# Linear attention with a gated feed-forward: wo's parts loaded a round ahead, the query pass's loads in written order, and the last product in two sets of columns

## Chip, cores and metric

The kernel runs on one core of a Trainium2 chip. The metric is the device time of one execution in microseconds (us); smaller is better. Times are compared as medians of several runs, and one further execution was recorded by the hardware profiler.

## The reference

S = 2048 tokens, D = 1024, H = 32 heads of 32, F = 3584, all in fp32.

```python
xn = layernorm(x)
q, k, v = heads(xn @ wqkv)
phi_q = concat(softmax(q @ w_phi), softmax(-q @ w_phi))      # per head, phi_k alike
kv  = einsum("bhsf,bhsd->bhfd", phi_k, v);  z = sum over s of phi_k
o   = (phi_q @ kv) / (phi_q @ z + 1e-6)
s   = o @ wo
g   = silu((silu(xn @ w1) * (xn @ w3)) @ w2)
out = x + s * g
```

## The kernel before

Every large product runs on TensorE (PE) in a reduced-width fp32 form. Each operand is split into a high and a low half, `split()`: ACT casts the high half (line 92), DVE subtracts to get the low half (line 93). A product is then three passes, high by high, high by low, low by high (`PASSES`, line 88). Two-by-two blocks are multiplied with seven products instead of eight (`ORDER`, line 59): A11, A12, S2, S1, S3, S4, A22, which accumulate in three PSUM banks a, b and c. Each of the seven is 12 matmuls of 128x512 here. Bank b is used by A11, S2, S3 and A22 one after the other, and c by S1 and S4, and the partial sums in between are read out of the bank. So PE's S2 waits for ACT's copy of A11, S3 for ACT's copy of S2, S4 for ACT's copy of S1, and A22 for DVE's addition after S3 or S4.

The stages follow one another: layer norm and the gate and up products with side work (to about 1117 us; the products of line 666), two K/V passes (c = 0 and 1, `heads`, products of line 951, to 1452 us), the query pass (c = 2, `query_heads` and `query_product`, line 1025, to about 1605 us), the down product (line 1430, to 2143 us) and the attention with the output product (`attend`, `out_half`, line 1594, to the end).

A K/V pass and the query pass have eight rounds each (`pos`), one for each pair of token tiles. A round is the seven products; after each of them (steps j = 0 to 6) the generator `steps()` issues side work:

- at j = 0 the seven operands `xo` of the next round, 512 KB each (`reload`, line 629);
- in the K/V passes one of 16 parts of wo, by `wo_split(c, k, j, halves)`: at j = 0 the load of the raw part from the input (`wo_raw`, 256 KB, line 1208), at j = 4 its split into two `wo_half`, at j = 6 their stores to `wo_d` in DRAM (line 1214);
- in some rounds the fetches of the next pass's weights, 2 MB each (`fetch`, line 169: `op3B`, `op3T` and so on);
- in the query pass the first loads of w2 (`bo`, `load_b`, line 1166) at the places named in `B_LOADS`.

In `heads`, k is copied out of bank b by ACT (line 957), v's parts by ACT (968 after S2, 972 after S1), then added by DVE (line 974 after S4); `kv_run` accumulates K'V in the bank `pkv` (line 907), by 64 small products between S2 and S1 of the next round. `kv_out` transposes the result by DVE into `kvz` (line 1128), and gives back two steps that are run at the ends of later products: `store` (lines 1139 and 1142) and `turned`, the small product `pz` (line 1133). In `query_heads` ACT copies q out of the banks (line 1093), POOL and DVE subtract the maxima and minima (lines 994 and 995), ACT takes the exponentials (998) and issues the store of the features to `e_d` (999). `rho_out` (line 1032) stores rho of a round, the ratios of its feature sums.

Order: in the K/V and query passes only PE's order is the written one (`in_order(ENG.PE)`); ACT, DVE, POOL and SP are placed by the framework's scheduler. From the last query round on, all engines are in written order. Loads and stores are issued mostly by SP, the feature stores by ACT.

The output product takes, for each of 16 token tiles, two halves of 512 columns with 24 matmuls of 128x512 each. A half is multiplied by the gate by DVE (`gate_mul`, line 1602), added to x (`gate_add`, line 1606; by GpSimd, and for the last tile by DVE) and stored (`store_out`, line 1610).

Of the kernel before, what the change touches and what calls it, by code (L numbers as in the profile page):

```python
# [27 lines left out]
def tile_kernel(ctx: ExitStack, tc: tile.TileContext, x, wkT, wqT, wv, wphi, wo, w1, w3, w2, out):  # L28
# [1006 lines left out]
    def query_last(i, xo, wb):  # L1035

        bank, rho, q, feats, late = {}, small.tile([P, 2, 2, 16], F, name="rho"), {}, {}, []
        parts = first_parts(ahead.pop(0))

        def kept(n, pb):  # L1040
            q[n] = work.tile([P, 512], F, name="q", tag="w")
            nc.scalar.copy(q[n], pb)

        def added(n, pb, j, c, room):
            nc.vector.tensor_add(q[n], pb, q[n])
            feats[n] = query_features(i, j, c, q.pop(n), rho, nc.gpsimd, room, True)
            feats[n][0]()

        for b, an, bn in ORDER:
            pb = query_product(bank, b, an, bn, xo, wb)  # L1050
            if an == "A11":
                kept("00", pb)
                ahead[1] = load_h(0, 1)
            elif an == "A12":
                early = e_room()
                added("00", pb, 0, 0, early[:, 0])
                next(parts)
            elif an == "S2":
                kept("01", pb)
                feats["00"][1]()  # L1060
                feats["00"][2]()
                ready.append(next(parts))
                parts = second_parts(*ready[0])
            elif an == "S1":
                kept("11", pb)
                next(parts)
            elif an == "S3":
                added("11", pb, 1, 1, early[:, 1])
                next(parts)
            elif an == "S4":  # L1070
                room = e_room()
                added("01", pb, 0, 1, room[:, 0])
                feats["11"][1]()
                ready.append(next(parts))
                parts = first_parts(ahead.pop(1))
                next(parts)
            else:
                feats["10"] = query_features(i, 1, 0, pb, rho, nc.vector, room[:, 1], True)
                feats["10"][0]()
        return {1: lambda: (ready.append(next(parts)), feats["11"][2]()), 3: lambda: feats["01"][1](), 5: lambda: feats["10"][1](),  # L1080
                7 + 5: lambda: feats["01"][2](),
                14 + 5: lambda: (feats["10"][2](), rho_out(i, rho), feats.clear())}

    def query_heads(i, first, xo, wb, steps):

        bank, rho = {}, small.tile([P, 2, 2, 16], F, name="rho")
        for b, an, bn in ORDER:
            pb = query_product(bank, b, an, bn, xo, wb)
            if late_z:
                z_add(late_z.pop())  # L1090
            if an in ("A11", "S2", "S1"):
                t = work.tile([P, 512], F, name="q", tag="w")
                nc.scalar.copy(t, pb)
                if an == "A11":
                    q00 = t
                elif an == "S2":
                    q01 = t
                else:
                    q11 = t
            elif an == "A12":  # L1100
                nc.vector.tensor_add(q00, pb, q00)
                early = e_room()
                query_features(i, 0, 0, q00, rho, nc.gpsimd, early[:, 0])
            elif an == "S3":
                nc.vector.tensor_add(q11, pb, q11)
                query_features(i, 1, 1, q11, rho, nc.gpsimd, early[:, 1])
            elif an == "S4":
                nc.vector.tensor_add(q01, pb, q01)
                late = e_room()
                query_features(i, 0, 1, q01, rho, nc.gpsimd, late[:, 0])  # L1110
            else:
                query_features(i, 1, 0, pb, rho, nc.vector, late[:, 1])
                rho_out(i, rho)
            if an == "S1" and first:
                kv_run(*pend)
                pend[2].clear()
                rooms_ev.clear()
                out_now.extend(kv_out(1, pkv))
            next(steps)
            if out_now and not first:  # L1120
                out_now.pop()()

    def kv_out(c, pkv):
        kvz = work.tile([P, 512], F, name="kvz", tag="w")
        kva, zt, zs = kvz[:, :8 * DH], kvz[:, 8 * DH:], zsum[1:]
        zsum.clear()
        for n in range(2):
            nc.vector.transpose(kva[:, P * n:P * n + P].rearrange("p (m d) -> p m d", d=DH), pkv[:, :, DH * n:DH * n + DH])

        def turned():  # L1130
            pz = ps.tile([P, 512], F, name="pz", tag="kv", bufs=1)
            for n in range(4):
                nc.tensor.matmul(pz[32 * n:32 * n + 32, :256], ones, zs[n // 2][:, n % 2 * 256:n % 2 * 256 + 256],
                                 start=True, stop=True, skip_group_check=True)
            nc.vector.tensor_scalar_add(zt[:64], pz[:64, :256], 1e-6)
            nc.vector.tensor_copy(zt[64:], pz[64:, :256])

        def store():
            nc.sync.dma_start(kv_d[:, :, :, c].rearrange("j f s m d -> (j f) s (m d)"),
                              kva.rearrange("p (s n) -> p s n", s=2))  # L1140
            for n in range(4):
                nc.sync.dma_start(z_d[n // 2, c].rearrange("(a g) n -> a (g n)", a=2)[n % 2:n % 2 + 1], zt[32 * n:32 * n + 1])

        return [store, turned]

# [54 lines left out]
    BANKS = {"a": 2, "b": 3, "c": 2}  # L1202
    pend = None
    ready, ahead = [], {}
    def wo_split(c, k, j, halves):
        if j == 0:
            halves.append(work.tile([P, 512], F, name="wo_raw", tag="w"))
            nc.sync.dma_start(halves[0], wo[k * P:(k + 1) * P, c * 512:(c + 1) * 512])
        elif j == 4:
            halves.extend(work.tile([P, 512], R, name="wo_half", tag="w") for _ in range(2))  # L1210
            split(halves[1], halves[2], halves[0])
        elif j == 6:
            for u in range(2):
                nc.sync.dma_start(wo_d[c][k][:, u], halves[1 + u].bitcast(F))

    in_order(ENG.PE)
    B_LOADS = ((3, 5), (4, 2), (4, 5), (5, 2), (5, 5), (6, 1), (6, 3), (6, 5))
    NEXT = ({0: 2, 1: 3, 2: 4, 3: 5, 4: 6}, {0: 2, 1: 3, 2: 4, 3: 5, 6: 6}, {})
    for c in range(3):
        wbn, last = {}, c == 2  # L1220
        if last:
            close("spare")
            bpa = pool("ra", 1, side="right")
        order = range(len(pairs))[::-1] if c == 1 else range(len(pairs))
        for pos, i in enumerate(order):
            nxt, end = {}, pos + 1 == len(pairs)

            def steps():
                halves = []
                for j in range(7):  # L1230
                    if j == 0:
                        if pos in (3, 4) and not last:
                            wbn.update(fetch(3 + c, pos - 3))
                        if not end:
                            nxt.update(reload(order[pos + 1]))
                    if not last:
                        wo_split(c, pos, j, halves)
                    if last and (pos, j) in B_LOADS:
                        m = B_LOADS.index((pos, j))
                        load_b(0, m // 2, (m % 2,))  # L1240
                    if end and j in NEXT[c]:
                        wbn.update(fetch(3 + c, NEXT[c][j]))
                    if last and pos + 2 == len(pairs) and j == 5:
                        ahead[0] = load_h(0, 0)
                    yield

            if last and end:
                in_order(ENG.SP, ENG.PE, ENG.Activation, ENG.DVE, ENG.Pool)
                late_features = query_last(i, xo, wb)
            elif last:  # L1250
                query_heads(i, pos == 0, xo, wb, steps())
            else:
                pend = heads(pos == 0, end, end and c == 1, xo, wb, steps(), pend)
            xo = xo if end else nxt
# [361 lines left out]
    for t in range(NT):  # L1616
# [31 lines left out]
        store_out(t, 0)  # L1648
        if count:
            lows.append(attend(t + 1, 0, count))  # L1650
        prev = out_half(t, 1, lambda: count and lows.append(attend(t + 1, 1, count)))
        for c in range(2):
            if count:
                lows[c].pop(0)()
            if t + 4 >= EARLY:
                z_sums(t + 4, c)
        lows = sum(lows, [])
    gate_mul(NT - 1, 1, prev)
    gate_add(NT - 1, 1, True)
    store_out(NT - 1, 1)  # L1660
    in_order()
    close("ps4", "rb", "acc", "q", "work", "small", "misc", "ra", "rw", "edge_r", "edge_l")

# [34 lines left out]
```

## Time and profile before

| | us |
|---|---|
| median of 3 runs | 2351.45 (2351.18 to 2353.81) |
| profiled execution | 2350.86 |
| span of its trace | 2349.1 |
| mean granted PE clock | 0.998 |
| PE's idle time before line 951's and 1025's products, and pz | 6.9 |
| last matmul's start to the end of the span | 4.8 |

The profiled execution is longer than its span by 1.8 us, the start and end that the trace does not show. The idle time in the fifth row is the sum of the waits that the list of PE's waits shows for those lines. In the profile's lists, "PE bankb L951 <- ACT k L957: 3.5, 1, 3.5" reads: PE's matmuls of line 951 into bank b waited for ACT's operation of line 957, 3.5 us in total, once, the longest 3.5. In a timeline a row is the start, the duration, the engine, the line, the operation with what it writes and reads, and the number of instructions in the group. A row of windows has, after the stretch and its length, the busy time of PE, weight loads, DVE, ACT and POOL with their counts, then the granted PE clock, the DMA engines' busy share and GB/s.

### The profile page before, as it was taken

What the parts mean: (1) busy time and instruction counts of PE and PEld (TensorE: products, weight loads), DVE (VectorE), ACT (ScalarE), POOL (GpSimd) and SP (SyncE); (2) the same over time, 40 slices, a digit from 0 to 9 for tenths busy, and PEclk for the clock granted to TensorE, in tenths of its full rate; (3) what the DMA queues carried; (4) which work ended last, traced back from release to release, by engine and by line L of the source; (5) the groups of instructions that cost most, each with busy time, mean ns of one, the idle gap of its engine ahead of it and who ended that gap; (6) DMA issues with size and microseconds to landing.
All of it is one profiled execution on the core that took longest, in us unless ns stands there. A gap on an engine that the chain in (4) does not pass through costs nothing.

```text
span 2349.1 us, 33851 instructions
## 1 busy us (share of the span) xinstructions
PE 2323.7 (99%) x12730; PEld 1900.2 (81%) x12730; DVE 1821.3 (78%) x2852; ACT 888.8 (38%) x1561; POOL 257.0 (11%) x208
## 2 busy tenths in 40 slices
PE   8999999999999999999999999999999999999999
PEld 6878877788888888888787887878888888887887
DVE  8878788885688888874577777778688888887784
ACT  6445444443345555543222122334433333353000
POOL 1000000000000000000000000332022222211652
PEclk9999999999999999999999999999999999999999
DMA  3456799997778888876978878996634554379863
GB/s 128 160 194 224 244 305 370 346 321 222 239 283 309 298 287 296 293 243 220 372 263 284 299 257 319 322 355 234 214 132 157 199 186 135 130 251 275 237 184 104
DMA packets 302740, 580.94 MB, mean 247 GB/s; under 512 B 24680, under 2 KB 156912, under 8 KB 299888
## 3 DMA queue, kind: packets, MB, share of 16 engines
q1 hardware_dynamic: 296240, 555.70, 70.2%
q10 hardware_dynamic: 6336, 23.07, 2.4%
q8 instruction: 100, 1.64, 0.3%
q14 instruction: 64, 0.52, 0.1%
HBM read 375.78 MB, written 202.91 MB: 246 GB/s over the span
## 4 chain that ended last, share of the span: by engine, by line
PE 89%; DMA 6%; DVE 2%; ACT 1%; issue 0%; POOL 0%; SPq 0%; ACTq 0%; POOLq 0%
PE bankb L666 26%; PE bankc L666 13%; PE bankb L1430 13%; PE bankc L1430 6%; PE bankb L951 6%; PE banka L666 6%; PE pm L1594 5%; PE banka L1430 3%; PE bankc L951 3%; PE bankb L1025 2%; PE banka L951 1%; DMA acc<-e_d 1%; DMA wo_raw<-in_wo 1%; PE bankc L1025 1%; DMA h_d<-h 1%; PE pkv L907 1%
## 5 line engine op out<-in xcount | busy, mean ns | idle before, releaser
L93 DVE TENSOR_TENSOR bo<-rw,bo 128x512 fp32r<-128x512 f32 x329 | 226.0, 688 | 145.9 <-ACT bo L92 145.6
L1430 PE MATMUL bankb<-bo,as 128*128 128x512 f32 x960 | 235.2, 389 | 0.0
L92 ACT CAST bo<-rw 128x512 fp32r<-128x512 f32 x329 | 202.3, 618 | 22.9 <-DMA wkv_d0B<-w2o 4.6
L1430 PEld LDWEIGHTS bankb<-bo,as 128*128 128x128 f32 x960 | 180.2, 188 | 37.7
L994 POOL TENSOR_TENSOR eq<-q,mm 128x512 f32<-128x512 f32 x24 | 25.2, 1050 | 1523.4 <-DVE mm L992 1495.5
L666 PE MATMUL bankb<-op0S,bo 128*128 128x512 f32 x672 | 166.7, 397 | 3.6 <-ACT u L702 2.8
L666 PE MATMUL bankc<-op0S,bo 128*128 128x512 f32 x672 | 162.1, 390 | 0.0
L666 PE MATMUL bankb<-op1S,bo 128*128 128x512 f32 x672 | 161.3, 389 | 0.0
L666 PE MATMUL bankc<-op1S,bo 128*128 128x512 f32 x672 | 161.3, 389 | 0.0
L666 PE MATMUL bankb<-op0A,bo 128*128 128x512 f32 x672 | 159.3, 391 | 1.1 <-ACT op0A L765 0.8
L1594 PE MATMUL pm<-wos,oT 128*128 128x512 f32 x672 | 158.3, 392 | 1.1 <-issue 0.9
L1430 PE MATMUL bankc<-bo,as 128*128 128x512 f32 x624 | 158.5, 389 | 0.2 <-DVE acc L1444 0.2
L666 PE MATMUL bankb<-op1A,bo 128*128 128x512 f32 x672 | 157.9, 390 | 0.0
L666 PEld LDWEIGHTS bankb<-op0S,bo 128*128 128x128 f32 x672 | 126.2, 190 | 36.4 <-issue 4.9
L1594 PEld LDWEIGHTS pm<-wos,oT 128*128 128x128 f32 x672 | 125.4, 188 | 29.4 <-issue 2.2
L666 PEld LDWEIGHTS bankb<-op1A,bo 128*128 128x128 f32 x672 | 125.8, 188 | 28.1 <-DVE u L710 2.1
L666 PEld LDWEIGHTS bankc<-op0S,bo 128*128 128x128 f32 x672 | 125.6, 188 | 27.3 <-issue 1.2
L666 PEld LDWEIGHTS bankb<-op0A,bo 128*128 128x128 f32 x672 | 125.4, 188 | 27.5 <-ACT op0A L765 1.0
L666 PEld LDWEIGHTS bankc<-op1S,bo 128*128 128x128 f32 x672 | 126.1, 188 | 26.2
L666 PEld LDWEIGHTS bankb<-op1S,bo 128*128 128x128 f32 x672 | 126.1, 188 | 26.2
L1430 PEld LDWEIGHTS bankc<-bo,as 128*128 128x128 f32 x624 | 117.0, 188 | 24.9 <-DVE acc L1444 0.6
L717 ACT ACTIVATE h<-bankb 128x512 f32<-128x512 f32 x56 | 33.5, 598 | 236.8 <-PE bankb L666 236.8
(291 smaller groups left out, 4394.6 us busy)
## 6 DMA issues: line engine op xcount, KB each, us to landing
rw<-in_w SPq DMA_DIRECT2D x112, 512.0 KB, 5.5
hr<-h_d SPq DMA_DIRECT2D x56, 512.0 KB, 5.5
h_d<-h SPq DMA_DIRECT2D x108, 256.0 KB, 5.7
xoS<-xo_d0S SPq DMA_DIRECT2D x44, 512.0 KB, 5.4
xoS<-xo_d1S SPq DMA_DIRECT2D x44, 512.0 KB, 5.5
xoA<-xo_d0A SPq DMA_DIRECT2D x33, 512.0 KB, 5.9
xoA<-xo_d1A SPq DMA_DIRECT2D x33, 512.0 KB, 5.1
e_d<-eq ACTq DMA_DIRECT2D x32, 512.0 KB, 6.6
```

Of the source, the lines that this page charges most:

```text
L92: nc.scalar.copy(hi, src)
L93: (by or nc.vector).tensor_sub(lo, src, hi.bitcast(F))
L666: nc.tensor.matmul(bank[b], bos[tb, f][bn][:, w, k], ao[an][:, u, k], start=first and n == 0, stop=LAST[b] == an and n == 11, skip_group_c ...
L717: nc.scalar.activation(h1, bank["b"], AF.Silu)
L907: nc.tensor.matmul(pkv[sl, m], v[:, 4 * m + h], e[:, :, 4 * m + h], start=first and m == 0, stop=last, skip_group_check=True)
L951: nc.tensor.matmul(bank[b], xo[an][:, u, k], wb[bn][:, w, k], start=an in ("A11", "A12", "S1") and n == 0, stop=LAST[b] == an and n == 11, ...
L994: eng.tensor_sub(e[:, 0], p3, mm[:, 0, :].unsqueeze(2).to_broadcast([P, 16, DH]))
L1025: nc.tensor.matmul(bank[b], xo[an][:, u, k], wb[bn][:, w, k], start=an in ("A11", "A12", "S1") and n == 0, stop=LAST[b] == an and n == 11, ...
L1430: nc.tensor.matmul(bank[b], t[:, u, pos + k], bos[kb, bn, k][:, w], start=first and n == 0, stop=LAST[b] == an and n == 5, skip_group_chec ...
L1594: nc.tensor.matmul(p, oTs[t, h][:, a, k], wos[c, 4 * h + k][:, b], start=n == 0, stop=n == 3 * ND - 1)
```

## The change

1. wo's parts. Part n + 1 is loaded at j = 4 of round n (parts 0 and 1 at j = 3 and 4 of round 0), split at j = 1 and stored at j = 2 of its own round, so that the load stands most of a round ahead of the split. Part 0 is split at j = 5 and stored at j = 6 of round 1.
2. The query pass. SP is put in written order together with PE. The w2 loads are no longer single parts at the places of `B_LOADS` but pairs at j = 5 of rounds 2 to 5. The store of rho is put after the next round's S4 (in the last round after S1). `kv_out` gives back four steps instead of two, so that its store comes two products later and `turned` stays where it was.
3. The last half of the last tile. It is done as two sets of 24 matmuls of 256 columns, each with its own multiplication, addition and store of 128 KB.

```diff
@@ query_last, query_heads
             elif an == "S1":
+                rho_out(*rhos.pop())
                 kept("11", pb)
...
+            if an == "S4" and rhos:
+                rho_out(*rhos.pop())
...
                 query_features(i, 1, 0, pb, rho, nc.vector, late[:, 1])
-                rho_out(i, rho)
+                rhos.append((i, rho))
@@ kv_out
-        return [store, turned]
+        return [store, lambda: None, lambda: None, turned]
@@ wo_split and the passes
-    def wo_split(c, k, j, halves):
-        if j == 0:
-            halves.append(work.tile([P, 512], F, name="wo_raw", tag="w"))
-            nc.sync.dma_start(halves[0], wo[k * P:(k + 1) * P, c * 512:(c + 1) * 512])
-        elif j == 4:
-            halves.extend(work.tile([P, 512], R, name="wo_half", tag="w") for _ in range(2))
-            split(halves[1], halves[2], halves[0])
-        elif j == 6:
-            for u in range(2):
-                nc.sync.dma_start(wo_d[c][k][:, u], halves[1 + u].bitcast(F))
+    wo_raws = {}
+
+    def wo_part(n):
+        return wo[n % 8 * P:(n % 8 + 1) * P, n // 8 * 512:(n // 8 + 1) * 512]
+
+    def wo_split(n, j):
+        new, now = ({3: 0, 4: 1} if n == 0 else {4: n + 1}).get(j), (((1, n),) if n else ()) + (((5, 0),) if n == 1 else ())
+        if new is not None and new < 16:
+            wo_raws[new] = [work.tile([P, 512], F, name="wo_raw", tag="w")]
+            nc.sync.dma_start(wo_raws[new][0], wo_part(new))
+        for at_, m in now:
+            if j == at_:
+                wo_raws[m].extend(work.tile([P, 512], R, name="wo_half", tag="w") for _ in range(2))
+                split(wo_raws[m][1], wo_raws[m][2], wo_raws[m][0])
+            elif j == at_ + 1:
+                raw_part, hi, lo = wo_raws.pop(m)
+                for u, h in enumerate((hi, lo)):
+                    nc.sync.dma_start(wo_d[m // 8][m % 8][:, u], h.bitcast(F))
...
-    B_LOADS = ((3, 5), (4, 2), (4, 5), (5, 2), (5, 5), (6, 1), (6, 3), (6, 5))
...
+            in_order(ENG.PE, ENG.SP)
...
-                        wo_split(c, pos, j, halves)
-                    if last and (pos, j) in B_LOADS:
-                        m = B_LOADS.index((pos, j))
-                        load_b(0, m // 2, (m % 2,))
+                        wo_split(8 * c + pos, j)
+                    if last and 1 < pos < 6 and j == 5:
+                        load_b(0, pos - 2)
@@ the last product
-        prev = out_half(t, 1, lambda: count and lows.append(attend(t + 1, 1, count)))
+        prev = None if last else out_half(t, 1, lambda: count and lows.append(attend(t + 1, 1, count)))
...
-    gate_mul(NT - 1, 1, prev)
-    gate_add(NT - 1, 1, True)
-    store_out(NT - 1, 1)
+    for u in range(2):
+        cs = slice(512 + 256 * u, 768 + 256 * u)
+        p = ps.tile([P, 512], F, name="pm", tag="mm", bufs=3)[:, :256]
+        n = 0
+        for k in range(ND):
+            for a, b in PASSES:
+                nc.tensor.matmul(p, oTs[NT - 1, k // 4][:, a, k % 4], wos[1, k][:, b, 256 * u:256 * u + 256], start=n == 0, stop=n == 3 * ND - 1)
+                n += 1
+        g, xr = gs[NT - 1][:, cs], xrs[(NT - 1) % 2][:, cs]
+        nc.vector.tensor_mul(g, p, g)
+        nc.vector.tensor_add(g, g, xr)
+        nc.sync.dma_start(out[(NT - 1) * P:, cs], g)
```

How instructions stand now is shown at three places. A row is a line, an operation, and what it writes and reads; "x2" is two alike in a row. ACT from round 0 to round 1 of the first K/V pass (`wo_half` is a part's high half, `k` the copy of A11, the copies into `ev` at 968 and 972 those of S2 and S1), before:

```order
L972 COPY ev<-bankc 128x512
L114 ACTIVATE ev<-ev 128x1024
L92 CAST wo_half<-wo_raw 128x512
L957 COPY k_9993<-bankb 128x512
L968 COPY ev<-bankb 128x512
L972 COPY ev<-bankc 128x512
L114 ACTIVATE ev<-ev 128x1024
```
and after the change:

```order
L972 COPY ev<-bankc 128x512
L114 ACTIVATE ev<-ev 128x1024
L957 COPY k_9989<-bankb 128x512
L92 CAST wo_half<-wo_raw 128x512
L968 COPY ev<-bankb 128x512
L972 COPY ev<-bankc 128x512
L114 ACTIVATE ev<-ev 128x1024
```
The cast stood ahead of the copy of k of round 1; now it stands between that copy and the copy of S2.

SP at the end of the first K/V pass, rounds 6 and 7 (`op3T` and `op3B` are the 2 MB fetches, `xoS` and `xoA` reloads, `wo_d` the stores of a split part), before:

```order
L629 DMA xoA_11201<-xo_d1A_94 128x1024
L629 DMA xoA_11203<-xo_d1A_95 128x1024
L629 DMA xoS_11205<-xo_d1S_96 128x1024
L169 DMA op3T_11035<-wkv_d2T_117 128x4096
L1208 DMA wo_raw<-in_wo 128x512
L169 DMA op3T_11061<-wkv_d2T_118 128x4096
L169 DMA op3T_11112<-wkv_d2T_119 128x4096
L169 DMA op3B_11128<-wkv_d2B_120 128x4096
L169 DMA op3T_11147<-wkv_d2T_121 128x4096
L1214 DMA wo_d_7_133<-wo_half 128x512 x2
```
and after the change:

```order
L1219 DMA wo_raw<-in_wo 128x512
L629 DMA xoS_10873<-xo_d1S_99 128x1024
L629 DMA xoA_10875<-xo_d1A_100 128x1024
L629 DMA xoA_11203<-xo_d1A_94 128x1024
L629 DMA xoA_11205<-xo_d1A_95 128x1024
L629 DMA xoS_11207<-xo_d1S_96 128x1024
L169 DMA op3T_11035<-wkv_d2T_117 128x4096
L169 DMA op3T_11065<-wkv_d2T_118 128x4096
L1227 DMA wo_d_7_133<-wo_half 128x512 x2
L169 DMA op3T_11118<-wkv_d2T_119 128x4096
L169 DMA op3B_11134<-wkv_d2B_120 128x4096
L1219 DMA wo_raw<-in_wo 128x512
```
The load of part 7 has left the fetches and stands five rows and more ahead of them; part 8's load now stands between them, and the stores of part 7 have moved ahead of the last three fetches.

SP in rounds 2 and 3 of the query pass (`bo` are w2's parts, `rho_d` the store of rho), before:

```order
L629 DMA xoA_13123<-xo_d1A_94 128x1024
L1166 DMA bo<-w_d0B_143 128x1024
L629 DMA xoA_13125<-xo_d1A_95 128x1024
L1166 DMA bo<-w_d0B_143 128x1024
L629 DMA xoS_13127<-xo_d1S_96 128x1024
L629 DMA xoS_13129<-xo_d1S_97 128x1024
L1166 DMA bo<-w_d0T_144 128x1024
L629 DMA xoS_13131<-xo_d1S_98 128x1024
L1166 DMA bo<-w_d0T_144 128x1024
L629 DMA xoS_13133<-xo_d1S_99 128x1024
L1166 DMA bo<-w_d0T_145 128x1024
L1032 DMA rho_d<-rho 128x2x32
```
and after the change:

```order
L1032 DMA rho_d<-rho 128x2x32
L1171 DMA bo<-w_d0B_142 128x1024 x2
L629 DMA xoA_13129<-xo_d1A_94 128x1024
L629 DMA xoA_13131<-xo_d1A_95 128x1024
L629 DMA xoS_13133<-xo_d1S_96 128x1024
L629 DMA xoS_13135<-xo_d1S_97 128x1024
L629 DMA xoS_13137<-xo_d1S_98 128x1024
L629 DMA xoS_13139<-xo_d1S_99 128x1024
L629 DMA xoA_13141<-xo_d1A_100 128x1024
L1032 DMA rho_d<-rho 128x2x32
L1171 DMA bo<-w_d0B_143 128x1024 x2
L629 DMA xoA_13291<-xo_d1A_94 128x1024
```
The single loads that lay between reloads are pairs behind seven reloads and the store of rho.

More of the change, by code (lines that the diff above doesn't have):

```diff
@@ L1082, in query_last @@
                 14 + 5: lambda: (feats["10"][2](), rho_out(i, rho), feats.clear())}
+    rhos = []
     def query_heads(i, first, xo, wb, steps):
@@ L1228, in steps @@
             def steps():
-                halves = []
                 for j in range(7):
```

## The prediction

> **What bounds the kernel now.** I first read the busy shares: TensorE (PE) works 2323.7 of 2349.1 us, so only time in which PE stands still, and time behind its last product, can be won. Then the waits of PE, sorted by what ended them (line; us in total, times, longest), for the lines that the change touches:
>
> ```profile
> PE 2323.7 (99%) x12730; PEld 1900.2 (81%) x12730; DVE 1821.3 (78%) x2852; ACT 888.8 (38%) x1561; POOL 257.0 (11%) x208
> ...
> PE bankb L951 <- ACT k L957: 3.5, 1, 3.5
> PE bankb L951 <- DVE ev L974: 1.3, 2, 0.7
> PE bankb L1025 <- ACT q L1093: 0.8, 1, 0.8
> PE bankc L1025 <- ACT q L1093: 0.7, 1, 0.7
> PE pz L1133 <- DVE kvz L1128: 0.4, 1, 0.4
> ```
>
> These are one wait in the K/V passes for ACT's copy of k, two for DVE, one before the first pz, two in the query pass: 3.5 + 1.3 + 0.8 + 0.7 + 0.4 = 6.7 us of idle time. A wait costs PE more than its idle time where matmuls behind it also run stretched, so I priced each by the distance between starts in PE's timeline (start, us, then the group). The yardstick is a query round without a wait, 1492.46 to 1511.50 below: 19.04 us for 7 products of 12 matmuls, 2.72 us each and 226.7 ns per matmul.
>
> **Part 1, wo's loads one round ahead.** The largest wait is in round 1 of the first K/V pass (the page's timeline, one window with PEclk as the second last but one column, and the chain of waits):
>
> ```profile
> 1140.79 2.88 PE L951 MATMUL banka<-op2B,xoA 128*128 128x512 f32 x12
> 1147.18 4.54 PE L951 MATMUL bankb<-op2T,xoS 128*128 128x512 f32 x12 [3.50 <-ACT k L957]
> 1151.64 1.10 PE L907 MATMUL pkv<-ev 128*32 128x64 f32 x64
> 1292.38 2.88 PE L951 MATMUL bankb<-op3T,xoS 128*128 128x512 f32 x12
> 1295.19 1.10 PE L907 MATMUL pkv<-ev 128*32 128x64 f32 x64
> ...
> 1145.00:1150.00 5.00, 2.82 (x7) 2.25 (x8) 3.62 (x6) 1.10 (x2) 0.00 (x0) 0.70 1.00 331
> ...
> 1136.81 9.19 DMA wo_raw<-in_wo
> 1146.02 0.62 ACT wo_half L92
> ```
>
> S2 was due at 1140.79 + 2.72 = 1143.51; an undisturbed S2 is followed by pkv after 1295.19 - 1292.38 = 2.81, so pkv was due at 1146.32. It started at 1151.64: 5.32 us lost, 3.67 by the late start and 1.65 because S2's twelve matmuls took 4.46 us (granted clock 0.70 in that window). The chain says why: the load of wo_raw goes out at 1136.81 and lands 9.19 us later, and ACT's cast of it (L92) stands in ACT's order ahead of the copy of k (L957) that empties bank b. In the changed order the copy of k stands ahead of the cast, so the whole 5.32 us should go. The Trainium skill, "TensorE: Matmul & The Clock Gate", part on the HAM clock gate, has the clock halve after a window of about 3.4 us with too little work; the 0.70 behind an idle of 3.50 us agrees, and by that rule a gap cut to 2 us would already save the stretched matmuls too.
>
> The wait moves: the cast of part 1 now stands ahead of L968, the copy of S2, for which S3 waits. Two loads go out where one did; at the window's 331 GB/s the second 256 KB land 0.79 us after 1146.00, at 1146.8. Cast 0.62 and copy of about 0.6 end at 1148.0. S3 is due 3.88 us after pkv (1295.19 to 1299.07 below), at 1150.2: 2.2 us to spare. If both landed 3 us later, 0.8 would be lost. I take nothing here. Round 1 also splits two parts, so DVE has a second subtraction of 0.69: I take 0.3 lost, between 0 and 0.7.
>
> The last rounds of both K/V passes have the same cast behind the 2 MB fetches of the next operands:
>
> ```profile
> 1277.33 2.88 PE L951 MATMUL bankb<-op2T,xoS 128*128 128x512 f32 x12
> 1286.94 2.88 PE L951 MATMUL bankb<-op3B,xoA 128*128 128x512 f32 x12
> 1299.07 2.88 PE L951 MATMUL bankb<-op3T,xoS 128*128 128x512 f32 x12
> 1307.23 2.88 PE L951 MATMUL bankb<-op3B,xoA 128*128 128x512 f32 x12
> ...
> 1268.48 10.64 DMA wo_raw<-in_wo
> 1279.85 0.69 DVE wo_half L93
> ...
> 1442.37 2.88 PE L951 MATMUL bankb<-op3T,xoS 128*128 128x512 f32 x12
> 1452.06 0.65 PE L907 MATMUL pkv<-ev 128*32 128x64 f32 x32
> 1433.53 10.38 DMA wo_raw<-in_wo
> ```
>
> Pass 0: S3 to the next A11 took 9.61 us, undisturbed 8.16: 1.45 lost. Pass 1: S3 to pkv took 9.69 instead of 8.16 + 0.09: 1.44 lost. In both, wo_raw needed over 10 us, and DVE's half of the split (L93) came late into the chain that ends in L974, which empties the bank for A22. In the change part 7's load is issued in round 6, ahead of the fetches, and part 15's likewise; the split then stands where nothing waits for a DMA. I take all of 1.45 + 1.44. The pz wait goes too: DVE's transposes of kvz stand ahead of L974 in the changed order, 0.4.
>
> What is late next: part 8, for round 0 of pass 1. Its load is issued in round 7 of pass 0, right behind a 2 MB fetch, and its cast stands on ACT ahead of an exponential and the copy of S2:
>
> ```profile
> 1277.52 0.32 SPq L169 DMA_DIRECT2D op3B<-wkv_d2B  x1
> op3B<-wkv_d2B SPq DMA_DIRECT2D x1, 2048.0 KB, 16.6
> 1295.91 0.59 ACT L968 COPY ev<-bankb 128x512 f32<-128x512 f32 x1 [4.51 <-PE pkv L907]
> 1297.09 1.06 ACT L114 ACTIVATE ev<-ev 128x1024 f32<-128x1024 f32 x1 [0.59 <-DVE ev L112]
> ```
>
> That fetch was issued at 1277.5 and landed 16.6 us later, at 1294.1. Put part 8 behind it, with 0.7 for itself and 0.7 for two wo_d stores that now go ahead of the fetch: 1295.5. Cast 0.62, exponential 1.06, copy 0.59 end at 1297.8; S3 stood at 1299.07 and is due 1.45 earlier, 1297.62. So 0.2 lost; if the load takes as long behind its fetch as the slowest above (10.6 us) behind theirs and lands 2 us later, 2 us; if it overtakes, nothing. I take 0.4.
>
> **Part 2, the query pass.** SP issues in written order; w2's loads (bo, four tensors of two 512 KB parts) no longer mix into the reloads but stand behind them, one pair in each of rounds 2 to 5.
>
> ```profile
> 1492.46 2.88 PE L1025 MATMUL bankb<-op4B,xoA 128*128 128x512 f32 x12
> 1511.50 2.88 PE L1025 MATMUL bankb<-op4B,xoA 128*128 128x512 f32 x12
> 1530.90 2.88 PE L1025 MATMUL bankb<-op4B,xoA 128*128 128x512 f32 x12
> 1552.00 2.88 PE L1025 MATMUL bankb<-op4B,xoA 128*128 128x512 f32 x12
> 1524.39 10.27 DMA bo<-w_d0T
> 1534.74 0.33 ACTq L999
> 1500.00:1520.00 20.00, 20.00 (x90) 16.58 (x89) 15.87 (x29) 6.01 (x7) 6.24 (x7) 1.00 1.02 404
> ```
>
> Three rounds from 1492.46 to 1552.00 take 59.54 us instead of 57.12: 2.42 lost, all in the second and third. ACT's store of the features (L999) waits for a bo load of 10.27 us, and the copies of q stand behind it on ACT; the DMA engines are full (share 1.02 at 404 GB/s). In the change a round moves 7 reloads of 512 KB (3.67 MB), four feature stores of as much (2.1) and one pair of loads (1.05): 6.8 MB in 19.04 us, 358 GB/s, under the 404 that choked. I take 2.0 of 2.42; bounds 0, if the stores wait as now, and 2.42. rho's store, one product later, and the kv store two steps later are read a pass or more later. SP's order has a price: a reload now stands behind rho's and bo's issue. Reloads are issued about a round before use, so I cost that at nothing; without that cover each round would wait.
>
> **Part 3, the last product.** 24 matmuls of 512 columns, 24 x 226.7 = 5.44 us, become 48 of 256.
>
> ```profile
> L1594 PEld LDWEIGHTS pm<-wos,oT 128*128 128x128 f32 x672 | 125.4, 188 | 29.4 <-issue 2.2
> 19.58 1.91 PE L231 MATMUL pt<-ident,xt 128*128 128x128 f32 x16
> 1475.43 0.64 PE L1133 MATMUL pz<-zsum,consts 128*32 128x256 f32 x8
> 2344.69 0.69 DVE L1602 TENSOR_TENSOR acc<-pm,acc 128x512 f32<-128x512 f32 x1 [4.02 <-PE pm L1594]
> 2346.13 0.33 SPq L1610 DMA_DIRECT2D out<-acc  x1
> L1192 DVE TENSOR_TENSOR s<-hr,sm 128x256 f32<-128x256 f32 x56 | 23.7, 424 | 0.0
> ```
>
> The trace has no such matmul. Lower bound: half of 226.7, 113 ns, 5.44 us. Upper: each pair waits for its weight load, 188 ns, 9.0 us. The 16 transposes, each with its own weights, took at most 1.91/16 = 119 ns, so loads can follow at that pace: 120 ns, 5.76 us, 0.3 more. The Trainium skill gives a load of 128 columns as P/1.2, 107 ns ("TensorE: Matmul & The Clock Gate", LDWEIGHTS); by that the load would hide and the 0.3 fall away, though the row shows 188. Behind the last matmul, multiply and add take 0.42 instead of 0.69 each: 0.5 less; half the store's bytes, 128 KB at 404 GB/s: 0.3 less (0 to 0.3). The first set's share hides behind the second set. Net 0.5 gained, between 0.8 gained and 3.1 lost.
>
> **The sum.** 5.32 + 1.45 + 1.44 + 0.4 - 0.3 - 0.4 + 2.0 + 0.5 = 10.4 us. The profiled execution took 2350.86, span 2349.1 and 1.8 around it: 2340.5. The median of the runs, 2351.45, is 0.6 above the profiled one: **2341.1**.
>
> **Rivals.**
> A: the wait moves instead of going. In round 1 of pass 0 and round 0 of pass 1 the cast still stands ahead of an ACT copy that PE needs; part 8 lies behind a fetch. For it: landings of 9 to 11 us wherever fetches run. Against: 2.2 us to spare in the first. Both late by 2 us or so: 2341.1 + 4 = 2345.
> B: the query pass keeps its loss, or SP's order costs as much as the quieter DMA gains: 2343 (2.0 less), or 2345 if the written order loses another 0.3 in each of 8 rounds.
> C: matmuls of 256 columns go at the pace of the 188 ns loads: 9.0 - 5.76 = 3.2 more, 2344.3.
> D, the slower side: products of 256 columns lose the rate of the 512s. The fp32 transposes show 119 ns for 128 columns, so 238 for 256, and a plain fp32 product of the code is two matmuls in the trace (four of pz, eight records), 476: 48 x 476 = 22.8 us against 5.76, 17 more, 2358. It decides from 14 us upward, 410 ns a matmul, where the change is slower by over 0.2%. Against: no row shows a product of this kind slowed by its size.
> E: the change doesn't order what it says, since ACT, DVE and POOL are still placed by the scheduler and the waits come back elsewhere: 2350. Against: the built order has the copy of k ahead.
>
> **Chances.** 0.62 forecast, with its own range 2339.3 to 2343.3; A 0.15; B 0.10; C 0.05; D 0.04; E 0.04. About 0.2%, 4.7 us, is what can be told from no change. Faster by more than that (below 2346.75): forecast, C, B and most of A, 0.89. Same: E and the tail of A, 0.06. Slower: D and what I overlook, 0.05. The range must hold forecast, B, C and half of A: 2339.0 (all gains full, no new wait, and the best end) to 2346.0.
>
> **What would show it.** Right: no wait of bankb for k at 1143, S2 of round 1 directly behind A11 at granted clock 1; rounds 7 of both passes at 8.16 and 8.25 us over the same stretches; query rounds of 19.04 throughout, bo landing in under 10 us; last product 5.8 us. Wrong: a wait of S3 for ACT's L968 copy in round 1 of pass 0 or round 0 of pass 1 over 1 us (A), reloads that PE waits for in the query pass (B), starts 188 ns apart at the end (C) or above 400 (D).

## The result and the profile after

The changed kernel takes 2341.51 us (median of 4 runs, 2339.93 to 2342.56), the kernel before 2351.39 (4 runs, 2351.18 to 2353.81): a ratio of 0.996, 95% interval 0.9948 to 0.9972. That is 9.9 us less, where 2341.1 and 10.4 less were forecast. The profiled execution is the slowest of the four, 2342.56, but its span is 2339.0, 10.1 under that of before; 3.6 us of it lie outside the span, where other runs of both kernels have mostly 1.8. So the terms are compared inside the span.

First PE's waits of the page after, with the busy shares ahead of them (us in total, times, longest):

```profile
PE 2320.3 (99%) x12754; PEld 1901.1 (81%) x12754; DVE 1825.2 (78%) x2854; ACT 889.0 (38%) x1561; POOL 258.6 (11%) x208
...
PE bankb L951 <- DMA xoA<-xo_d0A: 0.5, 1, 0.5
PE bankb L951 <- ACT ev L968: 0.5, 1, 0.5
```

Of the five waits shown of before none is left. (L974, which one of them names, is DVE's addition after S3; the addition after S4 is L976.) Two new ones stand in the K/V passes, 0.5 us each: for a reload of xoA, and for L968, the copy of S2 that was named as late next. PE's timeline of round 1 of pass 0, and one window over it (PEclk is the last but two column):

```profile
1138.93 3.01 PE L951 MATMUL bankb<-op2B,xoA 128*128 128x512 f32 x12 [0.53 <-DMA xoA<-xo_d0A]
1141.79 2.88 PE L951 MATMUL banka<-op2B,xoA 128*128 128x512 f32 x12
1144.51 2.88 PE L951 MATMUL bankb<-op2T,xoS 128*128 128x512 f32 x12
1147.32 1.10 PE L907 MATMUL pkv<-ev 128*32 128x64 f32 x64
...
1151.20 2.88 PE L951 MATMUL bankb<-op2T,xoS 128*128 128x512 f32 x12
...
1143.00:1148.00 5.00, 5.00 (x68) 3.98 (x70) 4.86 (x8) 0.17 (x1) 0.00 (x0) 1.00 1.03 398
```

S2 starts 2.72 us after A12 and pkv 2.81 after S2, as in any undisturbed round, and the clock stays at 1.00: the 3.67 us of standing still and the 1.65 of stretched matmuls went together. ACT's timeline at the same place shows where its wait for wo now lies:

```profile
1141.98 0.59 ACT L957 COPY k<-bankb 128x512 f32<-128x512 f32 x1
1147.83 0.62 ACT L92 CAST wo_half<-wo_raw 128x512 fp32r<-128x512 f32 x1 [5.26 <-DMA wo_raw<-in_wo]
1148.36 0.58 ACT L968 COPY ev<-bankb 128x512 f32<-128x512 f32 x1
```

ACT still waits 5.26 us for a raw part of wo, but behind the copy of k and ahead of the copy of S2, which ends at 1148.94; S3 is due at 1151.20, so 2.26 us are to spare where 2.2 were estimated. Over both passes ACT's waits for wo_raw fell from 49.6 us in 15 to this:

```profile
ACT wo_half L92 <- DMA wo_raw<-in_wo: 11.2, 2, 5.9
```

The table gives each stretch as the distance between two starts of A11 (rounds), or as named, in the two profiles:

| stretch | before | after | difference | forecast |
|---|---|---|---|---|
| gate and up stage, to the first A11 | 1119.01 | 1119.20 | +0.19 | 0 |
| round 0 of pass 0 | 19.04 | 19.73 | +0.69 | 0 |
| round 1 of pass 0 | 25.67 | 20.42 | -5.25 | -5.32, with +0.3 for the second split |
| round 2 of pass 0 | 20.29 | 20.51 | +0.22 | 0 |
| last round of pass 0 | 21.75 | 20.29 | -1.46 | -1.45 |
| round 0 of pass 1 | 20.29 | 21.13 | +0.84 | +0.4 |
| round 1 of pass 1 (pz) | 21.54 | 21.09 | -0.45 | -0.4 |
| last round of pass 1 | 22.40 | 20.97 | -1.43 | -1.44 |
| query rounds 3 and 4 | 40.50 | 38.08 | -2.42 | -2.0 |
| last half, from its first matmul to the end of the span | 10.05 | 9.46 | -0.59 | -0.5 |
| down product, and the rest | | | -0.44 | 0 |

From round 2 of the query pass on, the rounds start 19.04 apart (rounds 0 and 1 take 19.98 and 19.84, before and after alike):

```profile
1485.82 2.88 PE L1025 MATMUL bankb<-op4B,xoA 128*128 128x512 f32 x12
1504.86 2.88 PE L1025 MATMUL bankb<-op4B,xoA 128*128 128x512 f32 x12
1523.90 2.88 PE L1025 MATMUL bankb<-op4B,xoA 128*128 128x512 f32 x12
1542.94 2.88 PE L1025 MATMUL bankb<-op4B,xoA 128*128 128x512 f32 x12
1561.98 2.88 PE L1025 MATMUL bankb<-op4B,xoA 128*128 128x512 f32 x12
```

The timeline of all engines at the end: the second set's 24 matmuls of 256 columns start at 2332.41 and those of the first at 2329.54, so 2.87/24 = 119.6 ns apart; multiply and add take 0.42 each.

```profile
2329.54 0.52 PE L1675 MATMUL pm<-late,oT 128*128 128x256 f32 x3
2332.41 0.52 PE L1675 MATMUL pm<-late,oT 128*128 128x256 f32 x3
...
2335.49 0.42 DVE L1678 TENSOR_TENSOR acc<-pm,acc 128x256 f32<-128x256 f32 x1 [1.99 <-PE pm L1675]
2335.95 0.42 DVE L1679 TENSOR_TENSOR acc<-acc,xr 128x256 f32<-128x256 f32 x1
```

### The profile page after: what moved, and what is told of

It is laid out like the page before. It is cut to its first block, busy times and chain, and to the rows that moved or that the text cites. A ratio compares the mean times of both kernels' runs of the same rounds, so it can differ in the third digit from the quotient of the medians.

```text
span 2339.0 us, 33900 instructions
## 1 busy us (share of the span) xinstructions
PE 2320.3 (99%) x12754; PEld 1901.1 (81%) x12754; DVE 1825.2 (78%) x2854; ACT 889.0 (38%) x1561; POOL 258.6 (11%) x208
## 4 chain that ended last, share of the span: by engine, by line
PE 93%; DMA 3%; DVE 2%; ACT 1%; SPq 1%; issue 0%; DVEq 0%; ACTq 0%
PE bankb L666 26%; PE bankb L1441 13%; PE bankc L666 13%; PE bankb L951 7%; PE bankc L1441 6%; PE banka L666 6%; PE pm L1605 5%; PE bankb L1025 4%; PE bankc L951 3%; PE banka L1441 3%; PE bankc L1025 2%; PE banka L951 2%; DMA acc<-e_d 1%; PE banka L1025 1%; DMA wo_raw<-in_wo 1%; PE pkv L907 1%
```

## The experiments

### The parts by themselves

Four kernels, each against the kernel before on one chip (median there 2350.53, 25 runs, 2348.89 to 2355.12). Part 1 alone puts `wo_split(n, j)` and its calls into the kernel before.

> The kernel before with part 1 of the change alone. If the three parts add up (my theory), the profile shows round 1 of pass 0 at 20.3 to 20.6 us instead of 25.67, its last round and the last round of pass 1 at 20.3 and 21.0 instead of 21.75 and 22.40, round 0 of pass 1 0.8 longer than in the kernel before, and the query rounds 19.40 and 21.10 still there; span 2341.5, 7.5 under the kernel before. Rival: the query pass's loss came from the same late DMAs of the K/V passes and goes with them; then the query rounds read 19.04 and the span is 2339.5.

Measured: 2342.96 us (2341.01 to 2344.56), ratio 0.9962 (0.9948 to 0.9977), 7.6 less. In its profile round 1 of pass 0 reads 20.43, the last rounds 20.29 and 20.97, round 0 of pass 1 21.10; query rounds 3 and 4 read 19.24 and 20.53, so 1.69 are still lost there. So a loss in the query pass is left when the K/V passes' loads are early; the rival falls. The span is 2342.5 rather than 2341.5: the output product takes 194.7, where the kernel before and the changed one take 193.4.

The next kernel tests the cause of the large wait by itself: the load of part 0 stays late, only its split is moved.

```diff
+        if (c, k) == (0, 0):
+            if j == 0:
+                first.append(work.tile([P, 512], F, name="wo_raw", tag="w"))
+                nc.sync.dma_start(first[0], wo[:P, :512])
+            return
+        if (c, k) == (0, 1) and j == 1:
+            first.extend(work.tile([P, 512], R, name="wo_half", tag="w") for _ in range(2))
+            split(first[1], first[2], first[0])
+        elif (c, k) == (0, 1) and j == 2:
+            for u in range(2):
+                nc.sync.dma_start(wo_d[0][0][:, u], first[1 + u].bitcast(F))
```

> The kernel before, with part 0 alone split one round later (j = 1 of round 1; its load stays where it was, all other parts as before). Theory: the large wait is the order of ACT, the cast of part 0 ahead of the copy of k, so round 1 falls from 25.67 to 20.3 to 20.6 us though the load lands as late as before, and nothing else moves: span 2344.0. Rival: the late DMA traffic itself holds PE in round 1 (operands or the load land late whatever ACT does); then the round stays above 23 us.

Measured: 2345.88 us (2343.74 to 2349.67), ratio 0.9978 (0.9968 to 0.9987), 4.7 less. SP's, PE's and ACT's timelines:

```profile
1138.66 0.33 SPq L1210 DMA_DIRECT2D wo_raw<-in_wo  x1
...
1145.99 2.88 PE L951 MATMUL bankb<-op2T,xoS 128*128 128x512 f32 x12
1148.80 1.10 PE L907 MATMUL pkv<-ev 128*32 128x64 f32 x64
...
1143.47 0.59 ACT L957 COPY k<-bankb 128x512 f32<-128x512 f32 x1
1149.52 0.59 ACT L968 COPY ev<-bankb 128x512 f32<-128x512 f32 x1 [5.46 <-PE pkv L907]
1152.88 0.59 ACT L972 COPY ev<-bankc 128x512 f32<-128x512 f32 x1 [2.77 <-PE bankc L951]
1153.36 0.62 ACT L92 CAST wo_half<-wo_raw 128x512 fp32r<-128x512 f32 x1
```

The load goes out even later than before (1138.66 against 1136.81) and takes as long (about 10 us), the cast stands behind three copies, and round 1 reads 20.44. So it was ACT's order, not the traffic. The last round of pass 0, untouched, lost 2.96 in this execution (wo_raw took 12.19 us) where the kernel before lost 1.46: that stall varies from one execution to the next, while round 1's 5.4 to 5.6 us were there in all three profiles that keep the old order (25.67, 25.89, 25.87).

Part 2 alone (SP's order, the pairs of loads, the late stores of rho and kv):

> The kernel before with part 2 of the change alone. Theory: query rounds all 19.04, K/V passes as before: span 2346.7, 2.4 under the kernel before. Rival: the query pass's loss stays when the pass is entered with the K/V passes' late loads; then rounds of 19.4 and 21.1 remain and the span is within 0.5 us of the kernel before.

Measured: 2350.47 us (2346.54 to 2353.71, 10 runs), ratio 0.9994 (0.9985 to 1.0004). No gain in the median, and the interval reaches from 3.5 less to 0.9 more, so 2.4 less is inside it. Its profile, of a late execution (span 2351.9), has query rounds 2 to 7 at 19.04; from the pass's first matmul to the down product's first it takes 154.06 us against 156.48. That execution lost time elsewhere, most of it in the output product (waits of PE):

```profile
PE bankb L951 <- ACT k L957: 3.6, 1, 3.6
PE pm L1598 <- DVE oT L1588: 3.3, 2, 3.1
```

From the output product's first matmul to the last half it takes 197.8 us, against 193.4 before and 193.4 changed. The chain of waits there says why (start, us, what): g's load is issued when two loads of features, of 13 and 14 us, have landed one after the other, and takes 10.78 us itself, and DVE's multiplication by g stands ahead of what PE waits for.

```profile
2160.13 14.05 DMA acc<-e_d
...
2174.20 10.78 DMA g<-g_d
...
2185.07 0.06 DVE g L1606
...
2185.68 0.69 DVE oT L1588
```

Part 3 alone:

> The kernel before with part 3 of the change alone. From the start of the last half's first matmul to the end of the span the kernel before has 10.05 us, the changed kernel 9.46. Theory: 9.4 to 9.5 here too and nothing else moves: span 2348.5; the median of the runs can't tell it from the kernel before. Rival: the 0.6 us came from the store's state of the queue at that moment and not from the halves; then the tail is within 0.2 us of 10.05.

Measured: 2350.86 us (2346.99 to 2354.86), ratio 0.9998 (0.9988 to 1.0007). The tail can be read from the profile alone: 9.45 us (2336.25 to 2345.7), as in the changed kernel. The span, 2345.7, is 2.8 lower than expected, mostly because in this execution pass 1's last round read 20.97 and query rounds 3 and 4 lost only 0.82, without a change in either: those stalls sometimes do not come.

### Together, without part 2, and two variants

Against the kernel before on one chip (2350.83, 10 runs, 2346.98 to 2353.00).

> The changed kernel once more, on the chip of the next three, for their times and for a second profile of it. Theory: round 1 of pass 0 at 20.4, last rounds 20.3 and 21.0, query rounds all 19.04 again, 8.5 to 10.5 us under the kernel before by the medians. What is new since the first runs: each profile so far has another short wait in the output product (0 in the kernel before, 0.3 and 0.5 in the changed one, up to 5 with part 2 alone), where a load of g lands late. If that is chance, it differs here from the first profile of the same kernel; if it belongs to the kernel, it is the same.

Measured: 2340.22 us (2339.85 to 2344.14), ratio 0.9959 (0.9947 to 0.9972). The rounds are as in the first profile, but round 0 of pass 0 reads 19.04 and there is no wait for xoA: that 0.69 was chance. Over all profiles that round reads 19.04 to 20.15, and 19.44 with part 3 alone, which leaves the K/V passes as they were. In the output product the 0.3 for po is gone, and the waits without a named releaser are 0.5 instead of 0.3; it takes 192.9. So these waits are chance at least in part.

> The changed kernel with part 2 (the query pass) undone. Part 2 alone left the median where it was though its query rounds all read 19.04. Theory A, its gain is real and is lost to the output product's wait by chance: this is 1.5 to 2.5 us slower than the changed kernel by the medians, with the loss in query rounds 3 and 4. Theory B, what the query pass gains is given back later, since the passes behind it wait for the same DMA queue: this is within 0.7 us of the changed kernel, with slower query rounds and a shorter output stage.

Measured: 2341.66 us (2339.53 to 2344.28), 1.4 over the changed kernel in the same runs; query rounds 3 and 4 read 19.20 and 20.25, 1.37 lost, and the output product takes 193.5. The sizes fit theory A (a little under its band); the two kernels' runs overlap, so it is the profile that carries it. Nothing in it is given back as theory B has it.

The next kernel loads part 8 ahead of the fetches.

```diff
-        new, now = ({3: 0, 4: 1} if n == 0 else {4: n + 1}).get(j), ...
+        new, now = ({3: 0, 4: 1} if n == 0 else {4: 7, 5: 8} if n == 6 else {} if n == 7 else {4: n + 1}).get(j), ...
```

> The changed kernel with wo's part 8 loaded in round 6 of pass 0, right after part 7 and ahead of the 2 MB fetches, instead of in round 7 between them. Theory: the load of part 8, 17.8 us long, is what makes S3 wait in round 0 of pass 1, so that round goes from 21.13 to 20.3 us; span 0.8 under the changed kernel, nothing else moves. Rival: S3 waits because ACT and DVE have too much to do between the passes; then the round stays above 20.9.

Measured: 2339.24 us (2339.07 to 2339.28), ratio 0.9951 (0.9939 to 0.9964). The round reads 20.30, and the 0.8 is gone. But the theory of why is not borne out. First the changed kernel (the load of part 8 from the chain of waits, then the timelines of ACT, DVE and PE; the round's A11 starts at 1281.34):

```profile
1273.74 17.82 DMA wo_raw<-in_wo
...
1291.58 0.62 ACT L92 CAST wo_half<-wo_raw 128x512 fp32r<-128x512 f32 x1 [5.93 <-DMA wo_raw<-in_wo]
1291.84 0.68 DVE L112 TENSOR_TENSOR ev<-mm,k 128x512 f32<-128x512 f32 x1
1292.55 1.06 ACT L114 ACTIVATE ev<-ev 128x1024 f32<-128x1024 f32 x1 [0.35 <-DVE ev L112]
1293.52 0.56 ACT L968 COPY ev<-bankb 128x512 f32<-128x512 f32 x1
1294.14 3.06 PE L951 MATMUL bankb<-op3T,xoS 128*128 128x512 f32 x12 [0.51 <-ACT ev L968]
```

Then the kernel with part 8 early (A11 at 1280.81):

```profile
1280.81 2.88 PE L951 MATMUL bankb<-op3B,xoA 128*128 128x512 f32 x12
...
1289.78 0.59 ACT L968 COPY ev<-bankb 128x512 f32<-128x512 f32 x1 [3.95 <-PE pkv L907]
1290.82 0.69 DVE L112 TENSOR_TENSOR ev<-mm,k 128x512 f32<-128x512 f32 x1
1291.54 1.06 ACT L114 ACTIVATE ev<-ev 128x1024 f32<-128x1024 f32 x1 [1.17 <-DVE ev L112]
```

In the changed kernel the cast is done at 1292.20, and the exponential (L114) still waits until DVE's subtraction L112 ends at 1292.52; the copy of S2 (L968) stands behind the exponential, and PE's S3 behind the copy. DVE's half of the split comes after L112 and holds up none of this. All eight profiles with part 8 loaded between the fetches say the same: the cast ends 10.40 to 10.86 us after the round's A11, L112 always 11.17 to 11.18, and S3 starts always at 12.79 to 12.80, where 12.13 would be due, however late the load was. In the kernel with part 8 early the copy of S2 stands ahead of the exponential, as in the kernel before, and S3 starts at 12.13. So the edit moved two things, the load and, by way of the scheduler, ACT's order, and it is the order that the 0.8 hangs on; the rival, ACT and DVE between the passes, comes nearer. A kernel with the late load and the copy ahead of the exponential and of the cast was not run.

The fourth tries the output product's wait:

```diff
+        if t and t + 1 < NT and t + 1 not in gs:
+            load_gate(t + 1)
         if t + 5 < NT:
             load_e(t + 5 if t else 4)
```

> The changed kernel with the loads of g in the output stage issued ahead of the next tile's feature loads instead of behind them. Theory: PE's waits in the output product (for DVE behind a load of g of 9 to 11 us) go, and the spread of the runs with them: from the start of the output product to the start of the last half 193.2 us or less instead of 193.4, median 0.5 to 1 under the changed kernel. Rival: the feature loads then come late, and PE waits for po instead: same or slower.

Measured: 2342.39 us (2339.94 to 2344.27), ratio 0.9966 (0.9954 to 0.9978): not under the changed kernel's 2340.22, and spread as widely. The output product takes 193.2, as the theory has it, but the changed kernel's second profile has 192.9 without this edit, and the wait of 0.3 for po is there again. The theory isn't borne out: what spreads the runs is not this order of loads alone.

### The small matmuls, the query pass's order, and part 8 once more

Against the kernel before on one chip (2351.03, 15 runs, 2348.99 to 2354.46). The last half in four sets of 128 columns (`512 + 128 * u`, four turns of the loop):

> The changed kernel with the last half in four sets of 128 columns (96 matmuls) instead of two of 256. It measures what bounds the small matmuls: at 256 columns they start 120 ns apart. If that is the pace of the weight loads (109 to 120 ns), 128 columns start as far apart, 96 x 115 = 11.0 us instead of 5.7, and from the start of the last half to the end of the span it takes 9.46 + 5.3 - 0.4 for the smaller tail = 14.4 us, the kernel 4 to 5 us slower than the changed one. If it is the columns, 57 to 65 ns apart, 6 us, and the tail is 9.2 to 9.5.

Measured: 2344.77 us (2344.26 to 2345.69). The first two sets in its timeline:

```profile
2328.89 0.44 PE L1675 MATMUL pm<-late,oT 128*128 128x128 f32 x3
2331.51 0.50 PE L1675 MATMUL pm<-late,oT 128*128 128x128 f32 x3
```

2.62/24 = 109 ns apart, and 14.1 us from there to the end of the span (2343.0), where 14.4 was expected. So a matmul of 128 columns costs nearly as much as one of 256: here something that doesn't depend on the columns sets the pace. Each of these matmuls has its own weight load, which is the likely one; no run separates it from other costs of a matmul. At 256 columns, 119.6 ns, the half of 226.7 and this floor nearly meet.

w2's loads at their old places, SP in written order:

> The changed kernel with w2's loads at the places of the kernel before (single 512 KB parts in rounds 3 to 6), SP still in written order. Theory: what helps the query pass is the written order, which keeps these loads from being drawn forward between the reloads of rounds 2 and 3; so query rounds stay at 19.04, time within 0.5 us of the changed kernel. Rival: the pairs at the end of a round matter; then rounds 5 and 6, with two and three loads, read 19.3 or more.

Measured: 2341.49 us (2340.32 to 2341.97), ratio 0.9959 (0.9945 to 0.9972), against 2341.51 and 2340.22 for the changed kernel on two other chips; query rounds 2 to 7 all read 19.04. It is the order that matters, not the pairs.

The pairs kept, SP's order left to the scheduler (`in_order(ENG.PE, ENG.SP)` taken out):

> The changed kernel with SP's written order in the query pass taken back, the loads still written as pairs. The scheduler again puts the loads between the reloads of rounds 2 and 3. Theory: rounds 3 and 4 lose 0.8 to 2.4 us together, as in the kernel before; 1 to 2 us slower than the changed kernel. Rival: the order is of no account, the rounds read 19.04.

Measured: 2345.25 us (2341.37 to 2346.28, 8 runs), ratio 0.9973 (0.9963 to 0.9983). Round 3 reads 23.55: 4.5 lost in one round, more than expected. PE's timeline, the list of ACT's waits in the query pass, and the chain of waits ahead of PE's:

```profile
1504.37 2.88 PE L1025 MATMUL bankb<-op4B,xoA 128*128 128x512 f32 x12
...
1520.79 4.55 PE L1025 MATMUL bankc<-op4B,xoS 128*128 128x512 f32 x12 [2.65 <-ACT q L1098]
...
1527.92 2.43 PE L1025 MATMUL bankb<-op4B,xoA 128*128 128x512 f32 x10
...
ACT q L1098 <- DMA xoS<-xo_d1S: 4.1, 1, 4.1
...
ACT q L1098 <- DMA bo<-w_d0B: 2.4, 1, 2.4
...
1506.62 13.09 DMA xoS<-xo_d1S
...
1519.78 0.33 ACTq L999
...
1520.15 0.59 ACT q L1098
```

The wait is the one of the kernel before: ACT's store of features (L999) waits for an earlier load, the copy of q stands behind it, and PE behind the copy. Why a store should wait for that load is not shown: the two move different data. In the changed kernel's profile the same list for that stretch has no wait of ACT for a load.

Part 8 early, once more:

> The kernel with part 8 loaded early once more, beside the others on one chip. Its five runs lay within 0.2 us of each other, 1.0 under the changed kernel's median, while the changed kernel's runs spread over 4.3 us. If the early load also takes away what spreads the runs, they lie within 0.5 us again and at 2339.0 to 2339.5; if that was chance, some come 2 to 4 us later, as the changed kernel's do, and only the 0.8 us of round 0 of pass 1 stands.

Measured: 2340.24 us (2339.41 to 2343.97), ratio 0.9958 (0.9945 to 0.9970). Round 0 of pass 1 reads 20.29 again, but two of five runs came 2 to 4 us later: the narrow spread was chance. This profile's span is 2.2 us over that of the first one of the same kernel, and the time lies in stages that the change doesn't touch: the first A11 starts at 1120.67, 1.6 later, with 3.0 us of PE waiting for one of ACT's L702 where the first had 1.7; 0.4 of that is made up for by the end of the query pass, and the down product takes 1.0 longer. Over all executions the spans of the changed kernel (9 of them) have a median of 2338.5, with part 8 early (10) 2337.5: the 0.8 of that round and little else. By these spans it is the fastest version here.

## Why the prediction was right, point by point

- **Round 1 of pass 0.** Right in place and size (5.32 forecast, 5.25 in the table); the experiment with part 0's split alone shows the cause, ACT's order, since the load was late there too. The wait did move to ahead of L968 and its slack was 2.26 us. With the 0.3 for the second split the sum had 5.02 for this round.
- **The second split.** 0.3 was taken for round 1. It reads 20.29 to 20.47 in all kernels with part 1, and round 2 reads 20.5 in all of them, 0.2 over the regular one. In the changed kernel's profile these 0.2 stand in the 64 small products of round 2, which take 1.24 us to the next start instead of 1.03: DVE's L120, which makes what they read, ends at 1168.13, after they began at 1167.61. That the extra split on DVE delays L120 is likely, but no run tests it.
- **Last rounds and pz.** 1.45, 1.44 and 0.4 forecast, 1.46, 1.43 and 0.45 found; all three came with part 1 alone. But these two last rounds are no fixed price: other profiles of the old order have 2.96, 1.25 and 1.67 in pass 0, and 1.45, 1.81 and none in pass 1. That the terms of one profile fitted the medians so well is luck in part.
- **Part 8 (rival A in one of its two places).** Named, but undersized: 0.4 taken, 0.84 found. The landing came where the sum had it, 10.2 us after the round's A11 (1291.56 less 1281.34) against 10.0. The step that failed is the path behind it: the sum went over ACT's cast, exponential and copy without a wait, while the exponential waits for DVE's L112, whether the load is early or late within what the profiles show. S3 then starts 0.67 late and its matmuls take 0.17 more. So the stall was in the right place, but it is one of ACT's order and not of the load.
- **The query pass.** The size was right (2.0 taken of 2.42; all 2.42 came), the reason only half. The sum argued that 358 GB/s per round lie under the 404 that choked. The changed kernel's windows there read

```profile
1490.00:1500.00 10.00, 10.00 (x46) 8.29 (x45) 7.17 (x14) 3.65 (x5) 2.06 (x2) 1.00 1.02 408
1500.00:1510.00 10.00, 10.00 (x46) 8.29 (x45) 8.67 (x14) 2.71 (x3) 4.17 (x4) 1.00 1.03 415
```

  so the DMA engines are as full as before (share 1.02 and 1.03) and PE doesn't wait. What counts is which load the waited-for store has ahead of it, and the experiment without SP's order shows that this order decides it. Eight profiles with SP's written order lose nothing in rounds 3 and 4; six without it lose 0.8, 1.4, 1.7, 2.4, 2.8 and 4.5. Rival B, a loss by the written order, didn't show: 19.04 everywhere.
- **The last product.** 120 ns forecast, 119.6 found; 0.5 forecast, 0.59 found. Rivals C (188 ns) and D (476 ns) fall by that number.
- **The whole.** The span fell by 10.1 where the sum had 10.4. That they lie so close is luck in part: 1.5 us of loss that the sum didn't have (0.19, 0.69 and 0.22 in the first three stretches where 0 was forecast, 0.44 at part 8) stand against 1.2 of gain that it didn't have either (0.44 in the down product and the rest, 0.42 in the query pass, 0.23 in round 1 and small ones). Rival E falls with the rounds. The parts alone gave 7.6 less for the first, and for the other two a difference too small for their spread. That the query part's gain shows in the profile and not in its own medians is explained for one execution (the late load of g), not for all ten.

## What to carry to other kernels

When one engine copies results out of a bank and also works on loaded data, read its order, not its load: a cast that waits for a DMA costs whatever stands behind it, and moving it behind the copy was enough here, with the load as late as before. An edit to a load can also change the order that a scheduler gives other engines, so compare the orders before you credit the load. Where a scheduler may place loads, it may draw them between those that a store or a copy waits for; here, writing that queue's order out ended the stall at no cost that shows, although the DMA engines stayed as full. A stall that hangs on the landing of a DMA has no fixed price: look at several profiles before you put one into a sum.

## What was not expected of the hardware

A matmul with its own weights starts 109 ns after the one before it at 128 columns, 119.6 at 256 and 226.7 at 512, though the weight loads are recorded as 188 to 192 ns long: the records overlap, and a record's length is no pace. The Trainium skill, "TensorE: Matmul & The Clock Gate", LDWEIGHTS, gives a load of P columns as about P/1.2 ns, an estimate of 107 ns for 128 columns; the 109 agree with it.

A stall of PE can cost more than its idle time, but not every stall does. Windows of the kernel without SP's order, behind the idle of 2.65 us, and of the one with part 0's late split, around an idle of 1.70 (PEclk is the last but two column):

```profile
1520.70:1525.20 4.50, 4.41 (x13) 3.51 (x14) 1.97 (x3) 0.89 (x2) 2.06 (x2) 0.62 1.01 335
```

```profile
1277.00:1283.00 6.00, 3.63 (x15) 2.39 (x14) 4.34 (x7) 1.10 (x2) 0.00 (x0) 1.00 1.01 433
```

Behind 2.65 us the twelve matmuls of S4 took 4.39 us to the next start instead of 2.72, much as behind the 3.50 us of the kernel before (4.46); behind 1.70 the clock stayed at 1.00. The same page of the Trainium skill, in the part on the HAM clock gate, has the clock fall after at least one idle window of about 3.4 us; here 2.65 us were enough, and the measurement decides. Nor does the length of the idle alone decide: at 59 us of the span PE has stood still for 2.79 us in the kernel before and for 2.84 us in the one with part 0's late split, and from 60 to 62 us the clock reads 0.50 in the first and 1.00 in the second.
